# Where split value units begin: tile 3 in place of tile 2, in a fused Fourier mixing and SwiGLU kernel

## The chip, the cores and the metric

The kernel runs on one NeuronCore of a Trainium2 chip. The metric is the device time of one execution in microseconds (us), given as a median of several runs. In the profile five units work side by side: PE (TensorE, matmuls), DVE (VectorE), ACT (ScalarE), POOL (GpSimd) and the DMA engines (in the kernel before PE was busy for 97% of the span, DVE for 75%, ACT for 63%, POOL for 86%). SP (SyncE) shows only DMA issues there. L735 means line 735 of the kernel.

## The reference

A two-dimensional Fourier transform whose real part is kept, then a SwiGLU block on each row:

```python
def _attn_ref(x):                        # x: (8, 3008, 256) float32
    X = np.fft.fft(x, axis=1)
    X = np.fft.fft(X, axis=2)
    return X.real.astype(np.float32)

def _moe_ref(x, w_gate, w_val, w_out):   # x: (24064, 256), d_ff = 1536
    g = x @ w_gate
    silu = g * (1.0 / (1.0 + np.exp(-g)))
    val = x @ w_val
    return (silu * val @ w_out).astype(np.float32)
```

## The kernel before

The transform is done with matmuls on sums and differences of input rows. Making these sums is called folding here. It is elementwise work, it belongs to POOL, and each batch has two groups of folds: A (128 row pairs) and C (the rest; two batches share a tile after the first ones). One group is 14 steps in two halves:

```python
    def fold_steps(eng, X, CE, BB, q, r, given=None):
        # [...]
        return [lambda: sd(0, Alu.add), lambda: sd(1, Alu.subtract), even, odd, ab, ce, bb]
```

The steps are handed out over units of the main loop, and loads are issued in time for them:

```python
    spread(("C", 1), 14, 6, 14)
    spread(("A", 1), 14, 15, 24)
    lo = 25
    for b in range(2, B, 2):
        u = slot[(b, 0)] - 1
        spread(("C", b), 14, lo, (lo + u) // 2)
        spread(("A", b), 14, (lo + u) // 2 + 1, u)
        # [...]
```

The main loop has 24 tiles of up to 512 columns and 12 units in a tile, so tile 2 is units 24 to 35. A column stands for a transformed row and its mirror image, so each unit makes two hidden values: `hp` from P Wp + Q Wq, and `hm` from the same with Q's sign turned. There are two ways to do a unit:

- A plain unit adds a third matmul, with `Wm`, to the same PSUM value for gate and for value: 6 matmuls. DVE makes both products.
- A split unit keeps P Wp and Q Wm of the value apart (`e` and `o`) and lets DVE build both signs from them. That is 5 matmuls, three DVE operations, and both products go to POOL.

```python
        g = psG.tile([P, T], F32, name="g")
        mm(g, Wp, 0, Pt, True, False)
        mm(g, Wq, 0, Qt, False, True)
        if split(u):
            e = psV.tile([P, T], F32, name="v")
            mm(e, Wp, 1, Pt, True, True)
            o = psV.tile([P, T], F32, name="v")
            mm(o, Wm, 1, Qt, True, True)
            sg = sgv.tile([P, T], F32, name="sgv")
            nc.scalar.activation(sg[:, :w], g[:, :w], AF.Silu)                       # L728
            # [...]
            stt(es[:, :w], bc[t][:, :w], w0[:, f:f + 1], e[:, :w], ...)              # L731
            vp = vvp.tile([P, T], F32, name="vv")
            stt(vp[:, :w], o[:, :w], -0.5, es[:, :w], ...)                           # L733
            vm = vvp.tile([P, T], F32, name="vv")
            stt(vm[:, w - 1::-1], o[:, :w], 0.5, es[:, :w], ...)                     # L735
            nc.gpsimd.tensor_tensor(hts[t][0][:, f, :w], sg[:, :w], vp[:, :w], ...)  # L736
            return
        # [... plain: two matmuls, Silu L743, product on DVE L744]
```

`part_b`, run one unit later, makes the mirrored gate (matmul L753, Silu L757 or L761) and the second product (L758 on POOL, or L762 on DVE). Output matmuls of the tile before (L676, 8 in each unit) fill PE in between. A tile with split units has one broadcast matmul at its start (L856), which marks its beginning in the trace.

The buffers that matter are `psV` (3 buffers in PSUM), `vv` (4) and `sgv` (4). Each split unit takes two of each.

```python
    SPLIT = (0, 2, 3, 5, 7, 9)
    SPLIT_END = (0, 1, 2, 4, 5, 7, 8, 10, 11)
    t_end = tile_of((B - 1) * H) + 1              # 21

    def split(u):
        return 2 <= u[0] < nT - 1 and u[1] in (SPLIT if u[0] < t_end else SPLIT_END)
```

## Time and profile before

| | before |
|---|---|
| median of its first 3 runs | 693.22 us (692.69 to 694.37) |
| span of the profiled run | 691.4 us |
| PE busy | 673.5 us, 4369 matmuls |
| POOL busy | 593.4 us |
| tile 2, from its broadcast to tile 3's | 35.4 us |

From the page of the kernel before, the busy time of each engine, its share of the span and its number of instructions:

```profile
PE 673.5 (97%) x4369; PEld 414.4 (60%) x4369; DVE 517.9 (75%) x925; ACT 433.4 (63%) x765; POOL 593.4 (86%) x577
```

PE is the bound, busy for 673.5 of 691.4 us. A change that gives it work costs time, unless PE stood still somewhere. So the question is where it stands still. From the timeline of PE in the kernel before (start in us, duration, what; in brackets the idle time just ahead of it and what ended it), tile 2's first line, every later line of the tile that has such a bracket, and tile 3's first line:

```profile
75.64 0.38 PE L856 MATMUL g<-Qt,sel 128*128 128x512 bf16 x1
...
87.39 0.38 PE L716 MATMUL g<-Pt,Wp 128*128 128x512 bf16 x1 [0.90 <-ACT sgv L757]
...
90.16 0.57 PE L716 MATMUL v<-Qt,Wm 128*128 128x512 bf16 x1 [1.97 <-DVE vv L735]
...
97.55 0.38 PE L716 MATMUL v<-Pt,Wp 128*128 128x512 bf16 x1 [1.64 <-DVE vv L735]
98.14 0.38 PE L716 MATMUL v<-Qt,Wm 128*128 128x512 bf16 x1 [0.22 <-DVE hm L762]
...
111.08 0.37 PE L856 MATMUL g<-Qt,sel 128*128 128x480 bf16 x1
```

The first three of these gaps are 4.5 us, and with the fourth 4.7 us. Behind the three large ones stands POOL. From its timeline in the kernel before, around the start of tile 2:

```profile
76.07 4.69 POOL L153 TENSOR_TENSOR SDf<-XA 128x1024 f32<-128x1024 f32 x2
80.71 1.10 POOL L156 TENSOR_TENSOR EOf<-SDf 128x512 f32<-128x512 f32 x1
...
85.44 1.26 POOL L736 TENSOR_TENSOR hp<-sgv,vv 128x512 bf16<-128x512 f32 x1
...
88.12 1.26 POOL L758 TENSOR_TENSOR hm<-sgv,vv 128x512 bf16<-128x512 f32 x1
89.66 2.35 POOL L153 TENSOR_TENSOR SDf<-XC 128x1024 f32<-128x1024 f32 x1 [0.28 <-DMA XA<-in_x_dram]
91.96 1.27 POOL L736 TENSOR_TENSOR hp<-sgv,vv 128x512 bf16<-128x512 f32 x1
93.18 2.37 POOL L153 TENSOR_TENSOR SDf<-XC 128x1024 f32<-128x1024 f32 x1
```

At 76.07 us, when tile 2 has begun, POOL only starts the second half of batch 1's A folds. The first product of tile 2 waits until 85.44. The list of waits of the kernel before between 70 and 106 us (who waited for whom: total us, times, longest) shows how that reaches PE:

```profile
DVE vv L733 <- POOL hp L736: 4.4, 2, 2.5
...
PE v L716 <- DVE vv L735: 3.6, 2, 2.0
ACT sgv L757 <- POOL hp L736: 3.6, 2, 2.2
...
DVE vv L735 <- POOL hp L736: 2.8, 1, 2.8
```

Read it backwards: PE wants a value buffer (`psV`) that DVE has not read, and DVE cannot write `vv` because POOL has not used the older ones. After the second gap comes one more loss. From the stretches of the kernel before (stretch; its length and for each engine busy us and instructions; granted PE clock; DMA share; GB/s):

```profile
88.20:90.20 2.00, 0.04 (x1) 0.04 (x1) 0.78 (x2) 0.60 (x1) 1.73 (x2) 1.00 0.39 123
90.20:91.00 0.80, 0.80 (x4) 0.40 (x4) 0.80 (x2) 0.00 (x0) 0.80 (x1) 0.51 0.56 85
91.00:92.00 1.00, 1.00 (x5) 0.55 (x4) 0.36 (x1) 0.00 (x0) 1.00 (x2) 0.50 0.68 115
```

PE is "busy" in the last two, but at half clock, so the 512-column matmuls start 0.43 us apart in place of 0.217 us.

### The profile page before, as it was taken

Reading aid. Unit: us, or ns where it says so; the run is one execution under the profiler, and the core shown is the slowest. Engines: PE = TensorE matmul, PEld = TensorE weight load, DVE = VectorE, ACT = ScalarE, POOL = GpSimd, SP = SyncE. Lnnn points to the kernel's source line nnn. Section 1 sums busy time; section 2 is a strip of 40 time slices with the busy share of each in tenths; the row PEclk is TensorE's granted clock in tenths of the full one; section 3 lists DMA queues with packets and bytes.
Section 4 is the critical chain, followed back from the end, with each engine's and each line's share of the span. In section 5 each row is a group of like instructions: output and inputs, shape, how many; then the busy total and the mean of one; then the engine's idle time right before and its main releaser. Section 6 shows DMA issues by size and latency. Waiting matters only on the chain.

```text
span 691.4 us, 13273 instructions
## 1 busy us (share of the span) xinstructions
PE 673.5 (97%) x4369; PEld 414.4 (60%) x4369; DVE 517.9 (75%) x925; ACT 433.4 (63%) x765; POOL 593.4 (86%) x577
## 2 busy tenths in 40 slices
PE   7999979999999999999999999999999999999997
PEld 5446645566556566566665656655665656656676
DVE  8896657677768777777777778777877787788862
ACT  7676546566556566565665656655666656656663
POOL 8998999999999999999997989998999555658920
PEclk9999999999999999999999999999999999999999
DMA  9656362332413313324134111125111011111112
GB/s 225 113 78 131 101 142 74 96 99 61 131 37 90 110 31 105 89 68 132 47 82 117 45 34 46 32 58 140 43 36 46 32 41 37 46 32 47 47 47 70
DMA packets 45567, 52.55 MB, mean 76 GB/s; under 512 B 6290, under 2 KB 33466, under 8 KB 45498
## 3 DMA queue, kind: packets, MB, share of 16 engines
q1 hardware_dynamic: 42314, 49.35, 26.2%
q0 software_dynamic: 3184, 2.36, 2.4%
q8 instruction: 34, 0.56, 0.4%
q14 instruction: 35, 0.29, 0.2%
HBM read 29.39 MB, written 24.65 MB: 78 GB/s over the span
## 4 chain that ended last, share of the span: by engine, by line
PE 85%; DMA 4%; DVE 4%; issue 3%; POOL 1%; SPq 1%; ACT 1%; ACTq 0%; POOLq 0%; DVEq 0%
PE o L676 33%; PE v L716 17%; PE g L716 15%; PE g L753 8%; PE v L753 4%; PE g L567 3%; PE v L567 3%; DVE vv L735 2%; DMA XC<-in_x_dram 2%; DMA XC_108<-in_x_dram 1%; SPq L139 1%; DMA XA<-in_x_dram 1%; DVE vv L733 1%; DMA out_dram<-ev 1%; PE g L856 1%
## 5 line engine op out<-in xcount | busy, mean ns | idle before, releaser
L736 POOL TENSOR_TENSOR hp<-sgv,vv 128x512 bf16<-128x512 f32 (+1 forms) x132 | 167.8, 1272 | 49.8 <-DVE vv L733 38.4
L758 POOL TENSOR_TENSOR hm<-sgv,vv 128x512 bf16<-128x512 f32 (+1 forms) x132 | 167.3, 1272 | 8.5 <-ACT sgv L757 8.1
L676 PE MATMUL o<-Wo,hp 128*128 128x256 bf16 (+2 forms) x1140 | 170.6, 274 | 0.0
L676 PE MATMUL o<-Wo,hm 128*128 128x256 bf16 (+2 forms) x1140 | 169.6, 273 | 0.0
L676 PEld LDWEIGHTS <-hp 128*128 128x128 bf16 (+2 forms) x1140 | 112.3, 99 | 70.9 <-issue 11.3
L676 PEld LDWEIGHTS <-hm 128*128 128x128 bf16 (+2 forms) x1140 | 111.9, 98 | 64.8 <-issue 5.5
L731 DVE SCALAR_TENSOR_TENSOR es<-bc,w_85,v 128x512 f32<-128x512 f32 (+1 forms) x132 | 98.2, 744 | 51.3 <-PE v L716 51.0
L744 DVE TENSOR_TENSOR hp<-sg,v 128x512 bf16<-128x512 f32 (+2 forms) x156 | 103.7, 665 | 31.2 <-ACT sg L743 30.8
L761 ACT ACTIVATE sg<-g 128x512 f32<-128x512 f32 (+2 forms) x156 | 91.1, 584 | 43.1 <-PE g L753 43.0
L762 DVE TENSOR_TENSOR hm<-sg,v 128x512 bf16<-128x512 f32 (+2 forms) x156 | 103.2, 662 | 18.7 <-ACT sg L761 8.6
L743 ACT ACTIVATE sg<-g 128x512 f32<-128x512 f32 (+2 forms) x156 | 90.9, 583 | 41.5 <-PE g L716 39.6
L757 ACT ACTIVATE sgv<-g 128x512 f32<-128x512 f32 (+1 forms) x132 | 78.9, 598 | 53.9 <-PE g L753 41.3
L716 PE MATMUL v<-Pt,Wp 128*128 128x512 bf16 (+2 forms) x288 | 107.9, 375 | 1.6 <-DVE vv L735 1.6
L716 PE MATMUL g<-Pt,Wp 128*128 128x512 bf16 (+2 forms) x288 | 108.3, 376 | 1.0 <-ACT sgv L757 0.9
L716 PE MATMUL g<-Qt,Wq 128*128 128x512 bf16 (+2 forms) x288 | 108.0, 375 | 0.5 <-DVE Qt L580 0.5
L753 PE MATMUL g<-Qt,Wm 128*128 128x512 bf16 (+2 forms) x288 | 108.1, 375 | 0.0
L733 DVE SCALAR_TENSOR_TENSOR vv<-v,es 128x512 f32<-128x512 f32 (+1 forms) x132 | 91.1, 690 | 22.5 <-POOL hp L736 4.6
L728 ACT ACTIVATE sgv<-g 128x512 f32<-128x512 f32 (+1 forms) x132 | 78.7, 596 | 44.8 <-PE g L716 34.9
L735 DVE SCALAR_TENSOR_TENSOR vv<-v,es 128x512 f32<-128x512 f32 (+1 forms) x132 | 89.8, 681 | 8.1 <-POOL hm L758 5.2
L716 PEld LDWEIGHTS <-Wp 128*128 128x128 bf16 x576 | 56.4, 98 | 41.1 <-issue 4.5
L682 ACT COPY ev<-o 128x512 f32<-128x512 f32 x90 | 52.8, 587 | 30.9 <-PE o L676 29.7
L153 POOL TENSOR_TENSOR SDf<-XA 128x1024 f32<-128x1024 f32 x28 | 66.0, 2364 | 3.4 <-DMA XC<-in_x_dram 2.6
(173 smaller groups left out, 736.0 us busy)
## 6 DMA issues: line engine op xcount, KB each, us to landing
out_dram<-ev SPq DMA_DIRECT2D x96, 128.0 KB
XA<-in_x_dram SPq DMA_DIRECT2D x32, 256.0 KB
XA<-in_x_dram SPq DMA_DIRECT2D x112, 64.0 KB
XC<-in_x_dram SPq DMA_DIRECT2D x105, 32.0 KB
XC<-in_x_dram SPq DMA_DIRECT2D x28, 120.0 KB
out_dram<-ev SPq DMA_DIRECT2D x12, 120.0 KB
out_dram<-ev SPq DMA_DIRECT2D x10, 112.0 KB
XA<-in_x_dram SPq DMA_DIRECT2D x1, 1024.0 KB
```

What stands on the lines that cost most here:

```text
L676: nc.tensor.matmul(ps[:n, j, :], hts[minus][:, f, c:c + n], Wo[:, f, :], start=(f == 0), stop=(f == nF - 1))
L716: nc.tensor.matmul(ps[:, :w], Wt[:, gv, fs], src[:, :w], start=start, stop=stop, skip_group_check=True)
L731: stt(es[:, :w], bc[t][:, :w], w0[:, f:f + 1], e[:, :w], op0=Alu.mult, op1=Alu.add)
L733: stt(vp[:, :w], o[:, :w], -0.5, es[:, :w], op0=Alu.mult, op1=Alu.add)
L735: stt(vm[:, w - 1::-1], o[:, :w], 0.5, es[:, :w], op0=Alu.mult, op1=Alu.add)
L736: nc.gpsimd.tensor_tensor(hts[t][0][:, f, :w], sg[:, :w], vp[:, :w], op=Alu.mult)
L743: nc.scalar.activation(sg[:, :w], g[:, :w], AF.Silu)
L744: nc.vector.tensor_tensor(hts[t][0][:, f, :w], sg[:, :w], v[:, :w], op=Alu.mult)
L753: nc.tensor.matmul(ps[:, :w], Wm[:, gv, f * P:(f + 1) * P], Qt[:, :w], start=False, stop=True, skip_group_check=True)
L758: nc.gpsimd.tensor_tensor(hts[t][1][:, f, :w], sg[:, :w], v[:, :w], op=Alu.mult)
L761: nc.scalar.activation(sg[:, :w], g[:, :w], AF.Silu)
L762: nc.vector.tensor_tensor(hts[t][1][:, f, w - 1::-1], sg[:, :w], v[:, :w], op=Alu.mult)
```

## The change

Its intent is to take POOL's split products out of tile 2, where POOL is late. All 12 units of tile 2 become plain. The whole diff:

```diff
-        return 2 <= u[0] < nT - 1 and u[1] in (SPLIT if u[0] < t_end else SPLIT_END)
+        return 3 <= u[0] < nT - 1 and u[1] in (SPLIT if u[0] < t_end else SPLIT_END)
```

## The prediction

> **What bounds the kernel now.** TensorE: the busy table gives PE 673.5 us of the 691.4 us span, and the chain of waits is 85% PE. The timeline has a 128x512 matmul every 0.217 us and a 128x256 output matmul every 0.1085 us. [...] From 107 us on, the list of waits has one PE wait on another engine, 0.4 us.
>
> Tile 2 is the exception. It runs from 75.64 to 111.08 us (starts of its and tile 3's broadcast matmul): 35.4 us. By work it needs 6 split units x (5 x 0.217 + 8 x 0.1085) + 6 plain units x (6 x 0.217 + 8 x 0.1085) + broadcast 0.2 + batch 1's transform (103.8 to 107.0, 3.2 us) = about 28.2 us. The missing 7.2 us:
> - PE idle (timeline): 0.90 us before 87.4 (on ACT), 1.97 before 90.16 (on DVE L735), 1.64 before 97.55 (same), and small ones: about 5 us.
> - After the second gap the stretches show the granted clock at 0.50 from 90.2 to 93.6, matmuls every 0.43 us: about 1.8 us lost. ([...] here 2 us of idle was followed by 3.5 us at half.)
>
> The root is POOL. It is late with batch 1's folds: at 76.07 it starts a second half (two 2.35 us subtractions, then smaller pieces) that was issued ahead of tile 2. Its first product of tile 2 (L736) starts only at 85.44, so vv and sgv buffers fill, DVE and ACT wait 2 to 3 us for them (list of waits, 70 to 106 us), PSUM stays unread, and PE stops.
>
> **What the change does.** Six units of tile 2:
> - POOL loses 12 products of 1.27 us: -15.3 us.
> - DVE loses 18 scalar-tensor-tensors (0.74 + 2 x 0.69 us a unit), gains 12 products of 0.67 us: -4.7 us.
> - PE gains 6 matmuls, loses the broadcast: +1.1 us.
> - ACT loses one 0.59 us copy.
>
> All of tile 2 is then plain, like tile 1, where PE was 100% busy from 50 to 75.6 us.
>
> **On the critical path.** PE's 1.1 us is all on it; POOL's 15 us matters only through the 7 us it cost PE. New tile 2: 72 x 0.217 + 96 x 0.1085 + 3.2 = 29.2 us against 35.4: -6.2 us. POOL must catch up by tile 3, about 105 us. It finishes batch 1's folds near 86.8 us, waits for the next XC load (landed about 89.6; issue follows PE progress, so unchanged), and needs 13.4 us for the eight steps issued before tile 3: about 103 us. That is in time by an estimated 2 us, so the stall shouldn't just move. The rest shifts.
>
> **Predicted time:** 687.2 us (-0.9%), range 685.6 to 689.4. Faster by over 2%: 0.01; within 2%: 0.98; slower by over 2%: 0.01.
>
> **What would show it.** Tile 3's broadcast matmul near 105 us; PE idle in tile 2 below 0.5 us; granted clock 1.00 from 85 to 100 us; no PE waits on L735 or L757 there; POOL idle 2 to 3 us before 90 us on a DMA; POOL busy down 15 us; PE matmuls +5; later tiles as long as before.
>
> **What would make it wrong.** The XC load comes later, POOL still folds when tile 3's products come, and the stall with its clock drop moves to tile 3 (then 690 to 694 us). Or the half clock has another cause than PE idle and stays (about 689 us). Slower is possible only by the 1.1 us of PE work, with the stall wholly moved.

Its terms are counts of matmuls and times read from the profile of before: 72 x 0.217 + 96 x 0.1085 + 3.2 = 29.2 us for tile 2 in place of 35.4 us, so -6.2 us. That idle time of PE brought the half clock on was the reading of what that profile shows once: 1.97 us of idle, then clock 0.50 from 90.2 to 93.6 us.

## The result, and the profile after

| | before | after |
|---|---|---|
| median, 4 runs each | 693.74 us | 687.67 us (687.24 to 688.74) |
| ratio | | 0.9916 (95% interval 0.9898 to 0.9935) |
| span of the profiled run | 691.4 us | 685.5 us |
| tile 2 | 75.64 to 111.08: 35.44 us | 75.91 to 105.18: 29.27 us |
| tile 3's broadcast to the end | 580.3 us | 580.3 us |

A ratio here is the mean time of one kernel's fast runs over that of the other's fast runs of the same rounds, so it is not quite the ratio of the quoted medians.

The last two rows locate the gain: all of it lies ahead of tile 3. Tile 2 is 6.17 us shorter. The profiled run lost 0.27 us of that in its first 76 us, which the change does not touch. That start-up part differs between profiled runs: tile 2 began anywhere from 75.6 us (before) to 77.5 us (a later run). In the four profiles where it began latest (deep_buf, after_again, end18 and end18_last3, 77.1 to 77.5 us) the mean granted clock was 0.993 in deep_buf, with 0.83 in its stretch from 10 to 20 us, and 0.997 in the others. Of the other ten, seven had 1.000, and three (before, tile8_plain, before_odd) had 0.997 or 0.998, with half clock in or behind a stall of PE after 76 us. Below, therefore, kernels are also compared by the time from tile 2's start to the end, which leaves the start out: 615.7 us before, 609.6 us after, and 609.5 us in a second profile of the changed kernel.

The page of the changed kernel, busy times:

```profile
PE 672.8 (98%) x4374; PEld 414.2 (60%) x4374; DVE 514.6 (75%) x919; ACT 432.9 (63%) x764; POOL 579.1 (84%) x565
```

There are five more matmuls, as counted (6 more, less the broadcast), and 12 fewer POOL instructions. PE's busy time still fell by 0.7 us: before, 3.40 us of it (90.2 to 93.6 us) was half-clock work, at clock 0.50. The timeline of PE after, tile 2's first line (it has no broadcast now) and tile 3's broadcast:

```profile
75.91 0.38 PE L716 MATMUL g<-Pt,Wp 128*128 128x512 bf16 x1
...
105.18 0.37 PE L856 MATMUL g<-Qt,sel 128*128 128x480 bf16 x1
```

The stretches of PE after (length; PE busy and matmuls; clock; DMA share; GB/s) cover tile 2 in the first two lines and tile 3 in the third. There is no gap and no half clock:

```profile
76.00:88.00 12.00, 12.00 (x79) 1.00 0.35 100
88.00:105.00 17.00, 16.98 (x115) 1.00 0.63 151
105.00:132.00 27.00, 26.95 (x176) 1.00 0.33 97
```

The timeline of POOL after shows the same folds, in one run, and what POOL does when they are through:

```profile
77.09 4.67 POOL L153 TENSOR_TENSOR SDf<-XA 128x1024 f32<-128x1024 f32 x2
...
89.98 4.68 POOL L153 TENSOR_TENSOR SDf<-XC 128x1024 f32<-128x1024 f32 x2 [2.02 <-DMA XC<-in_x_dram]
...
100.93 2.35 POOL L153 TENSOR_TENSOR SDf<-XC 128x1024 f32<-128x1024 f32 x1
107.91 1.21 POOL L736 TENSOR_TENSOR hp<-sgv,vv 128x480 bf16<-128x480 f32 x1 [4.63 <-DVE vv L733]
```

POOL is even later with batch 1's folds than before (77.09 against 76.07), but nothing waits for it. It is through with the next batch's first eight steps at 103.3 us, and then idles 4.63 us until tile 3's first product can be made. The stall did not move to tile 3.

### The profile page after: what moved, and what is told of

Same layout as the page of the kernel before. It is cut to its first block, busy times and chain, and to the rows that moved or that the text cites. A ratio compares the mean times of both kernels' runs of the same rounds, so it can differ in the third digit from the quotient of the medians.

```text
span 685.5 us, 13259 instructions
## 1 busy us (share of the span) xinstructions
PE 672.8 (98%) x4374; PEld 414.2 (60%) x4374; DVE 514.6 (75%) x919; ACT 432.9 (63%) x764; POOL 579.1 (84%) x565
## 4 chain that ended last, share of the span: by engine, by line
PE 89%; DVE 5%; issue 2%; POOL 2%; ACT 0%; DVEq 0%; ACTq 0%; POOLq 0%
PE o L676 34%; PE v L716 17%; PE g L716 16%; PE g L753 9%; PE v L753 4%; PE g L567 3%; PE v L567 3%; DVE vv L735 3%; DVE vv L733 1%; PE v L543 1%; PE g L543 1%; PE g L856 1%; PE g L421 1%; PE v L421 1%; PE o L430 0%
## 5 line engine op out<-in xcount | busy, mean ns | idle before, releaser
L736 POOL TENSOR_TENSOR hp<-sgv,vv 128x512 bf16<-128x512 f32 (+1 forms) x126 | 160.1, 1272 | 54.3 <-DVE vv L733 42.4
L758 POOL TENSOR_TENSOR hm<-sgv,vv 128x512 bf16<-128x512 f32 (+1 forms) x126 | 159.6, 1272 | 8.5 <-ACT sgv L757 8.1
L744 DVE TENSOR_TENSOR hp<-sg,v 128x512 bf16<-128x512 f32 (+2 forms) x162 | 107.9, 666 | 33.2 <-ACT sg L743 32.4
L731 DVE SCALAR_TENSOR_TENSOR es<-bc,w,v 128x512 f32<-128x512 f32 (+1 forms) x126 | 93.7, 744 | 50.5 <-PE v L716 50.3
L762 DVE TENSOR_TENSOR hm<-sg,v 128x512 bf16<-128x512 f32 (+2 forms) x162 | 107.4, 663 | 24.1 <-ACT sg L761 14.4
L761 ACT ACTIVATE sg<-g 128x512 f32<-128x512 f32 (+2 forms) x162 | 94.7, 585 | 45.6 <-PE g L753 45.4
L743 ACT ACTIVATE sg<-g 128x512 f32<-128x512 f32 (+2 forms) x162 | 94.4, 583 | 45.0 <-PE g L716 43.5
L757 ACT ACTIVATE sgv<-g 128x512 f32<-128x512 f32 (+1 forms) x126 | 75.3, 598 | 47.4 <-PE g L753 41.1
L728 ACT ACTIVATE sgv<-g 128x512 f32<-128x512 f32 (+1 forms) x126 | 75.1, 596 | 40.3 <-PE g L716 35.5
L733 DVE SCALAR_TENSOR_TENSOR vv<-v,es 128x512 f32<-128x512 f32 (+1 forms) x126 | 87.0, 690 | 17.6 <-PE v L753 1.0
L735 DVE SCALAR_TENSOR_TENSOR vv<-v,es 128x512 f32<-128x512 f32 (+1 forms) x126 | 85.7, 680 | 2.7 <-POOL hm L758 2.7
```

Source lines behind the costliest of these rows:

```text
L731: stt(es[:, :w], bc[t][:, :w], w0[:, f:f + 1], e[:, :w], op0=Alu.mult, op1=Alu.add)
L733: stt(vp[:, :w], o[:, :w], -0.5, es[:, :w], op0=Alu.mult, op1=Alu.add)
L735: stt(vm[:, w - 1::-1], o[:, :w], 0.5, es[:, :w], op0=Alu.mult, op1=Alu.add)
L744: nc.vector.tensor_tensor(hts[t][0][:, f, :w], sg[:, :w], v[:, :w], op=Alu.mult)
L758: nc.gpsimd.tensor_tensor(hts[t][1][:, f, :w], sg[:, :w], v[:, :w], op=Alu.mult)
L762: nc.vector.tensor_tensor(hts[t][1][:, f, w - 1::-1], sg[:, :w], v[:, :w], op=Alu.mult)
```

## The experiments

Theories and rivals, with their names in the expectations:

- Theory 1: PE stood still only in tile 2, because POOL could not give back `vv` and `sgv`. 1a says that the late folds of batch 1 did it. 1b says, more generally, that POOL had too much work there.
- Rival A: POOL is busy 86% of the time, and less work for it helps anywhere.
- Rival B: the load of the next batch, which lands near 89.6 us, held up the products queued behind it.
- Rival C: two more buffers would have done the same.
- Rival D: two split units side by side (2 and 3) made the stall.

The runs came in three groups of four. Each group shared one chip and its runs of the kernel before. Medians of before: 694.97, 694.31 and 694.45 us.

### tile8_plain: the same work taken from another tile

```diff
-        return 2 <= u[0] < nT - 1 and u[1] in (SPLIT ...
+        return 2 <= u[0] < nT - 1 and u[0] != 8 and u[1] in (SPLIT ...
```

> The kernel before, with tile 8 plain in place of tile 2 (split units in tiles 2 to 7 and 9 to 22). It removes exactly the same work from POOL, DVE and ACT as the change does and adds the same PE work, but in a tile where PE does not wait. Theory 1 (the gain is the removal of a PE stall that exists only in tile 2): the stall stays, PE pays for 5 more matmuls, about +1.1 us, so 694 to 695 us; tile 8 lasts 26.3 us, up from 25.25 us. Rival A (POOL is 86% busy, so 15 us less work for it gains wherever it is taken): about -6 us, 687 to 688 us.

Measured: 694.42 us, ratio 0.9983 (0.9958 to 1.0007). From tile 4's broadcast to tile 9's, which holds tile 8, it took 136.70 us against 135.92 us before: 0.8 us more, where 1.1 us was counted. Tile 2 stalled as before (36.9 us in this profile). Rival A's 6 us did not come, so it falls. The time alone does not resolve the 0.8 us.

### first3 and last3: three split units left in tile 2, early ones or late ones

```diff
-        return 2 <= u[0] < nT - 1 and u[1] in (SPLIT if ...
+        return 2 <= u[0] < nT - 1 and u[1] in ((0, 2, 3) if u[0] == 2 else SPLIT if ...
-        if f == 0 and split((t, SPLIT[0])):
+        if f == 0 and any(split((t, j)) for j in range(nF)):
```

and the same with `(5, 7, 9)`.

> The kernel before, with only the first three of tile 2's six split units (0, 2 and 3). Their products queue on POOL behind the late folds of batch 1 (done near 87 us). Theory 1a (these late folds are what holds the products up): the first two gaps of PE stay, 2 to 3 us of idle, with the half clock after them, so about 690 to 692 us. Rival B (what holds them up is the first subtraction of the next batch, which waits for its load until 89.6 us and stands in the queue ahead of the later products): only the products after unit 25 suffer, little idle is left, about 687 us. Rival A expects half of the gain, about 690.5 us, without any particular gap.

> The kernel before, with only the last three of tile 2's six split units (5, 7 and 9). Theory 1a: by their time POOL is through with batch 1's folds, and vv and sgv hold two units of lag, so PE idle in tile 2 is under 0.7 us, clock 1.00, tile 2 lasts about 28.8 us, total 687.0 to 687.8 us (0.4 us of PE less than with all of tile 2 plain). Rival B (load and next batch's subtractions hold products up): gap of 1 to 4 us before unit 9, 689 to 692 us. Rival A: half of the gain, about 690.5 us.

Measured: first3 691.05 us, ratio 0.9937 (0.9918 to 0.9956), tile 2 lasts 32.4 us. last3 689.16 us, ratio 0.9912 (0.9895 to 0.9930), tile 2 lasts 29.9 us. The list of PE's waits from 60 to 140 us, for first3:

```profile
PE v L753 <- DVE hp L744: 1.7, 1, 1.7
PE g L716 <- ACT sgv L757: 1.2, 1, 1.2
```

and for last3:

```profile
PE v L567 <- DVE vv L735: 0.8, 1, 0.8
```

The number of units and the work are the same in both, but the early ones cost about 2.5 us more of tile 2. The products that stand behind batch 1's late folds are what hurts most, as 1a says. In first3 the next batch's load was no limit: its first subtraction began at 90.33 us, right after a product.

last3 is a miss for 1a: tile 2 took 1.1 us more than the expected 28.8 us, and 689.16 us lies outside the 687.0 to 687.8 us of 1a and inside the 689 to 692 us of rival B. The timeline of POOL in last3 shows why:

```profile
90.17 4.69 POOL L153 TENSOR_TENSOR SDf<-XC 128x1024 f32<-128x1024 f32 x2 [1.56 <-DMA XC<-in_x_dram]
94.81 1.10 POOL L156 TENSOR_TENSOR EOf<-SDf 128x512 f32<-128x512 f32 x1
95.84 0.21 POOL L157 COPY EOf<-SDf 128x4 f32<-128x4 f32 x1
95.99 1.28 POOL L736 TENSOR_TENSOR hp<-sgv,vv 128x512 bf16<-128x512 f32 x1
```

Batch 1's folds were over at 88.6 us. POOL then waited 1.56 us for the load, and unit 5's product, whose `vv` was written by 90.2 us, stood behind the subtractions until 95.99 us. So rival B is right in a small way: the gap of 1 to 4 us before unit 9 did not appear, but PE lost the 0.8 us above. In the kernel before, POOL waited only 0.28 us for the load. The clock stayed at 1.00 in first3 (84 to 106 us) in spite of its gaps of 1.24 and 1.70 us, where a half clock was expected.

### deep_buf: the split kept, deeper buffers

```diff
-    sgp = ...(name="sg", bufs=3)
-    sgv = ...(name="sgv", bufs=4)
+    sgp = ...(name="sg", bufs=2)
+    sgv = ...(name="sgv", bufs=6)
-    vvp = ...(name="vv", bufs=4)
-    evp = ...(name="evO", bufs=4)
+    vvp = ...(name="vv", bufs=6)
+    evp = ...(name="evO", bufs=3)
```

> The kernel before, all splits kept, but vv and sgv with 6 buffers each in place of 4 (room from sg 3 to 2 and ev 4 to 3). One more split unit may lag behind before DVE and ACT stop. Rival C (only the depth of these buffers made the stall): nearly all of the 7 us come back, 686 to 687.5 us. Theory 1b (POOL has too much work between 76 us and tile 3, buffers only set when that is felt): the gap before 87.4 us vanishes, a later one remains or grows, PE idle in tile 2 between 1.5 and 4 us, total 688 to 692 us. [...]

Measured: 694.85 us, ratio 0.9994 (0.9972 to 1.0016). Tile 2 became 2.9 us shorter (32.57 us): the first two gaps are gone, and one of 2.11 us is left, with a half clock after it (0.50 from 100 to 102 us), much as 1b expected of this tile. But tile 5 became 2.9 us longer (31.36 us against 28.43), which neither theory foresaw, so that the time is outside both ranges (686 to 687.5 us for rival C, 688 to 692 us for 1b). From tile 2's start to the end it is 615.8 us, against 615.7 us before. The list of PE's waits of deep_buf from 165 to 194 us, and its stretches there (length; PE busy; clock; DMA):

```profile
PE g L567 <- POOL CEa L167: 0.3, 1, 0.3
PE g L567 <- POOL CEa L166: 0.3, 1, 0.3
PE o L676 <- POOL hp L736: 0.3, 1, 0.3
```

```profile
172.00:176.00 4.00, 3.33 (x25) 1.00 0.53 134
...
178.00:181.00 3.00, 3.00 (x13) 0.50 0.75 213
```

The transform of batch 2 now waits for its folds. These waits are only 0.9 us of the 2.9; the half clock behind them (177.97 to 181.38 us) is worth about 1.7 us more (an estimate, half of its length), so that the loss equals the gain is partly chance. Deeper buffers let POOL's debt be carried, not paid: it falls due when the next batch must be ready. Rival C falls, and 1b, though its time was missed, is the better wording of the theory. In the kernel before, from 75.64 to 178 us, when batch 2's transform is done, POOL was busy 100.2 of 102.4 us. In the changed kernel, from 75.9 to 172.2 us, it was busy 86.5 of 96.3 us. All of that slack lies ahead of 122 us: from there to 172 us POOL was busy 49.8 of 50.0 us, and the fold that batch 2's transform reads (`CEa`, L167) ended at 169.43 us, only 0.4 us before the matmul that reads it. The two smaller pools of this experiment (`sg` and `ev`) could have cost something too. No wait of PE names them.

### after_again and tiles23_plain: the control, and one step further

```diff
-        return 3 <= u[0] < nT - 1 and ...
+        return 4 <= u[0] < nT - 1 and ...
```

> The changed kernel as it is, as the control for the three others on the same chip. All theories: ratio to the kernel before 0.990 to 0.993, as in its first rounds (0.9916).

> One step further: split units begin at tile 4. In the changed kernel PE no longer waits in tile 3 (0.0 us of waits of PE on other engines from 76 to 132 us). Theory 1: nothing left to win there, PE pays 5 matmuls of 480 columns, about 1.0 us slower than the changed kernel on the same chip, ratio to before 0.992 to 0.994; tile 4's broadcast matmul starts about 1 us later. Rival A (less POOL work gains anywhere): as much again as the first step, about 6 us faster than the changed kernel.

Measured: after_again 687.71 us, ratio 0.9908 (0.9891 to 0.9924). tiles23_plain 687.46 us, ratio 0.9906 (0.9891 to 0.9921). The expected loss of 1 us did not show in the times. In the profiles, the way from tile 2's start to tile 4's broadcast is 0.7 us longer than with tile 3 split (57.74 against 57.05 us), and tile 4 is then 0.4 us shorter (25.15 against 25.53 us). To the end it is 609.8 against 609.5 us. So Rival A's further 6 us is refuted, and the price of a plain tile is less than counted. Two reasons were found in the traces. In the control PE waits 0.5 us in tile 4 for DVE's L735, and with tile 3 plain this wait is gone. The other is a late start that tiles 3 and 5 to 20, all with this set of split units, show, as follows.

From the timeline of the changed kernel (after_again), two split units side by side in tile 10, units 2 and 3, all engines:

```profile
305.98 0.68 DVE L735 SCALAR_TENSOR_TENSOR vv<-v,es 128x512 f32<-128x512 f32 x1
...
306.24 0.38 PE L716 MATMUL v<-Pt,Wp 128*128 128x512 bf16 x1
...
306.71 0.38 PE L716 MATMUL v<-Qt,Wm 128*128 128x512 bf16 x1
```

Elsewhere in this trace the next matmul mostly starts 0.217 us after one of 512 columns. The second of these starts 0.47 us after the first, just as DVE's read ends (306.66). The author takes this to mean that three value buffers are one too few for two split units in a row. In the profile of the changed kernel tiles 5 to 20 each show the same distance at their units 2 and 3 (0.47 or 0.48 us). In tile 3, with 480 columns, it is 0.41 us in place of 0.20, and tile 4 has the wait for L735 there (0.44 us). This 0.25 us does not appear in the list of waits, because PE counts as busy for most of it (the first matmul is shown until 306.62 us).

### end18 and end18_last3: more split units where POOL has room

```diff
-    t_end = tile_of((B - 1) * H) + 1
+    t_end = tile_of((B - 1) * H) - 2
```

on top of the change; end18_last3 also has tile 2's units 5, 7 and 9 split.

> The changed kernel with the denser split set (9 of 12 units in place of 6) from tile 18 in place of tile 21. The folds on POOL end near 518 us, and in tiles 18 to 20 POOL is busy only 55 to 75%. Theory 1, used the other way round (where POOL has room, a split unit saves PE one matmul and stalls nothing): 9 matmuls of 0.217 us less, 1.9 us faster than the changed kernel on the same chip, ratio to before 0.988 to 0.990. Rival A (more POOL work costs anywhere): 3 x 7.6 us more POOL work makes it slower by several us.

> As end18, and tile 2 split in its units 5, 7 and 9. Those three save PE 0.43 us net of the broadcast, but in the profile of last3 PE waited 0.8 us near the end of tile 2. So within 0.5 us of end18, either way; both theories say the same of this one, it is run as a candidate for the best version.

Measured: end18 688.10 us, ratio 0.9912 (0.9897 to 0.9926). end18_last3 688.41 us, ratio 0.9918 (0.9904 to 0.9933). Neither is faster than the control, so the expected ratio of 0.988 to 0.990 was missed. Tiles 18 to 21 together took 110.7 us from tile 18's broadcast to tile 22's, against 111.0 in the control: 0.3 us, where 9 matmuls of 0.217 us were saved. The denser set has five pairs of neighbours within a tile (the text below says four). In the trace of tile 18 its matmuls show three late starts of 0.25 to 0.29 us, where the control has one. The two more are nearly what the three saved matmuls of the tile are worth. The kernel got no faster, but 21 us more POOL work did not make it slower, which is again against Rival A.

### before_odd, after_odd, after_even, after_odd_all: no neighbours

```diff
-    SPLIT = (0, 2, 3, 5, 7, 9)
+    SPLIT = (1, 3, 5, 7, 9, 11)
```

on the kernel before and on the changed one; after_even with `(0, 2, 4, 6, 8, 10)`; after_odd_all with `t_end = nT` as well.

> The kernel before (split units from tile 2), with the six split units of a tile at 1, 3, 5, 7, 9, 11 in place of 0, 2, 3, 5, 7, 9. In the changed kernel each tile loses about 0.25 us where split units 2 and 3 stand side by side: the second one's last product waits until DVE has read the first one's, 3 value buffers being one too few for two split units. Rival D (tile 2's stall came from the neighbours 2 and 3, not from the amount of POOL work): tile 2 takes about 28.5 us, gain about 7 us in tile 2 and 0.25 us in each other one, so 682 to 683 us. Theory 1b (too much POOL work at that place): tile 2 still stalls by 3 to 6 us (it lasts 32 to 35 us); gain of about 0.25 us in each of some 18 tiles, ratio to before 0.992 to 0.996.

> The changed kernel with split units at 1, 3, 5, 7, 9, 11. If the 0.25 us belong to the neighbours, 18 tiles give back 0.25 us each: 4 to 5 us faster than the changed kernel, ratio to before 0.984 to 0.987; each of tiles 3 to 20 is 0.2 to 0.3 us shorter. From tile 2's start to the end 605 us, in place of 609.5. If a split unit after or before the transform of unit 4 costs as much, nothing changes (0.991).

> As after_odd with units 0, 2, 4, 6, 8, 10: no neighbours either, but unit 4 stands just ahead of the transform that most tiles have there, which wants value buffers. Between the changed kernel (0.991) and after_odd, 0.984 to 0.991. A separate theory, that any placement without neighbours is alike, puts it level with after_odd.

> after_odd with the odd set up to the last split tile: tiles 21 and 22 have 6 split units in place of 9, of which four pairs are neighbours. In end18 the denser set won only 0.3 us in three tiles, for 9 matmuls of 0.217 us saved, so it should be level with after_odd within 0.5 us.

Measured:

| run | median us | ratio (95%) |
|---|---|---|
| before_odd | 693.77 | 0.9987 (0.9969 to 1.0005) |
| after_odd | 688.90 | 0.9930 (0.9911 to 0.9949) |
| after_even | 687.60 | 0.9902 (0.9884 to 0.9920) |
| after_odd_all | 689.22 | 0.9924 (0.9908 to 0.9940) |

before_odd still stalls in tile 2 (33.3 us), within its expected range, so Rival D falls. Its gain in the other tiles did not come (a ratio of 0.992 to 0.996 was expected): tile 5 alone took 32.37 us, with a wait of PE of 2.39 us for POOL's L736 and a half clock behind it (512-column matmuls 0.42 us apart at 173.6 us). after_odd missed its expectation as well: 4 to 5 us were expected, and nothing was gained (610.8 us from tile 2's start to the end, against 609.5). Its trace says why. Most of its tiles are shorter, as expected (tile 8 24.94 us against 25.24, tile 7 28.12 against 28.43). But a few are longer: tile 5 took 30.69 us against 28.43, and tile 9 30.11 against 28.64. The timeline of PE in after_odd, the only line of tile 5 with a bracket:

```profile
166.67 0.28 PE L676 MATMUL o<-Wo,hp 128*128 128x256 bf16 x1 [2.40 <-POOL hp L736]
```

With a split unit at 11, the last product of tile 4 is still on POOL when tile 5's output matmuls want it. In all, PE waited 5.7 us for such products in after_odd, and the gain was spent on them. after_odd_all is level with after_odd, as expected.

after_even is inside its expected range, but it did not win the 0.25 us either: its tile 8 took 25.20 us. In its trace no unit of that tile has such a late start, but the first gate matmul behind the broadcast starts 0.26 us late (244.98 us); what it waits for was not looked into. Its tile 5 took 29.55 us, with a wait of 1.0 us for POOL's L736.

The set in the kernel ends at unit 9 and so leaves time. Six split units without neighbours in 12, and none in the last two, do not exist. No version tried is clearly faster than the changed kernel.

## Why the prediction was right

- **Time.** 687.2 us predicted (685.6 to 689.4), 687.67 us measured. That the two agree so closely is partly luck: the stalled tile 2, with the same instructions, took 35.44 us in the profile of before and 36.92 us in that of tile8_plain.
- **The sum.** Tile 2 was to take 29.2 us in place of 35.4 us. It took 29.27 us in place of 35.44 us.
- **What to see.** Tile 3's broadcast came at 105.18 us (near 105 predicted). PE had no wait on another engine in tile 2. The clock was 1.00. POOL idled 2.02 us on a DMA before 90 us. There were five more matmuls.
- **POOL's catching up.** The eight steps ended at 103.3 us (about 103 predicted). The time to spare was 4.6 us where 2 us were estimated, because tile 3's first product can only be made about 2.7 us after its broadcast.
- **The root.** The prediction named the late folds. first3 against last3 supports this, last3 adds a small part for the next batch's load and subtractions, and deep_buf widens it: between tile 2 and batch 2's transform POOL had nearly no time to spare, so the debt would have fallen due somewhere.
- **Too simple.** The prediction reckoned a plain unit as exactly one matmul dearer (1.1 us for a tile). Where no stall is involved, tiles23_plain and tile8_plain showed 0.3 to 0.8 us, and part of the difference is the 0.25 us that neighbouring split units lose.
- **Left open.** How much of the gain is the half clock was not measured by itself. In the profile of before, 3.4 us at half clock cost about 1.7 us of the 6.2 (an estimate, half of its length). What sets it off was not shown. Gaps of 1.97 us (before), 2.39 us (tile8_plain, before_odd) and 2.11 us (deep_buf) were followed by it. Gaps of 1.97 us (tile8_plain, before 91.21 us), 2.40 us (after_odd), and 1.24 and 1.70 us (first3) were not. In deep_buf it came once, at 177.97 us, where no wait of PE in the list from 165 to 194 us was over 0.34 us. So other executions of the kernel before may have had more or less. The recorded clocks say that most of the gain does not need it: in the second group, two runs of before with a mean clock of 0.999 took 693.00 and 693.51 us, and three of the changed kernel at 0.999 or 1.000 took 687.35 to 687.93 us. No run took the products from POOL alone, or moved batch 1's folds alone. That POOL and not DVE, which also lost work, leads the chain in tile 2 rests on the list of waits.

## What to carry to other kernels

This case suggests that work moved from the bounding engine to a helper pays only while the helper can repay it before the next hard date. Add up the helper's work between two such dates, not over the whole span. Here, with the helper in debt, deeper buffers moved the stall to a later date (deep_buf: tile 2 2.9 us shorter, tile 5 2.9 us longer), and taking work away removed it (tile 2 6.17 us shorter, tile 3's broadcast to the end the same 580.3 us). To weigh changes under 1%, compare runs from a mark in the trace that lies just ahead of the change, because the start-up part may vary by more than the effect: here tile 2 began at 75.6 to 77.5 us in 14 profiles.
